# Tables, running-sum rows and spreads laid out with an outer dimension of eight in an attention and spectral-mix kernel

## The chip, the core and the metric

The kernel runs on one core of one Trainium2 chip. The metric is the device time of one execution in microseconds. The core has a matrix engine (TensorE, PE in the profile, with its weight loads as PEld), a vector engine (VectorE, DVE), an activation engine (ScalarE, ACT), GpSimd (POOL) and SyncE (SP), which computes nothing here and issues transfers. Transfers between DRAM, and within the on-chip memory (SBUF), are carried out by 16 DMA engines, which all queues share.

## The reference

Two layers follow each other. The first is causal attention with a learned decay, for 8 batches, 8 heads, 576 tokens and 64 values a head:

```python
scores = scale * np.matmul(q, k.transpose(0, 1, 3, 2))
cum = np.cumsum(np.maximum(s, 0.0), axis=-1)
bias = -(cum[:, :, :, None] - cum[:, :, None, :])
scores = np.where(causal, -1000000000.0, scores + np.minimum(bias, 0.0))
attn = softmax(scores)            # as max, exp, sum
x = np.matmul(attn, v)            # heads side by side: (8, 576, 512)
```

The second takes the Fourier transform of x along the tokens, keeps 64 modes, multiplies each mode by a complex 512 x 512 matrix of its own (`w_r`, `w_i`), transforms back and applies a last dense layer:

```python
X = np.fft.rfft(x, axis=1)
Yr = einsum('bmd,mde->bme', Xr, w_r) - einsum('bmd,mde->bme', Xi, w_i)
Yi = einsum('bmd,mde->bme', Xr, w_i) + einsum('bmd,mde->bme', Xi, w_r)
y = np.fft.irfft(Y, n=S, axis=1)
u = x + y
out = u + np.maximum(u @ w_ch, 0.0)
```

`w_r` and `w_i` together hold 2 x 64 x 512 x 512 values in float32, 134 MB, and are by far the largest input. The output is 8 x 576 x 512 in float32.

## The kernel before

**Attention and the stream of weights.** The 64 heads and batches are worked on in 32 steps of two heads of one batch (`n` from 0 to 31; `g, b = divmod(n, 8)`). A step transposes q and k on TensorE (`transposes`, L347), computes scores (`scores`, L381), their exponentials on ScalarE, the product with v (`av`, L416), and the forward transform of the result by a small matmul with a table (`fft`, L450). The decay enters through an additional row of the transposed q: row D of the tile `qt` holds minus eight times the running sum of `s` for the step's two heads, which meets a row of ones in `kt`.

The running sums are computed once, for all 64 heads and batches, by a scan on VectorE (L292) into `ncum_sb`, 64 partitions x 576 values in bfloat16. `cum_rows` (L336) brings two rows of them into `qt`, one transfer per step, issued by SP one step ahead. For steps 0 and 1 the row comes straight from `ncum_sb` (L345); for the other 30 it comes from a copy in DRAM, `ncum_dram`, which one transfer at L586 writes.

While attention runs, GpSimd issues the transfers of weights, q, k and v (`load`, L239, all at L243): they convert float32 to bfloat16 or float16 on the way. The weights come in pieces of 8 modes x 128 rows of the inner dimension, real and imaginary apart: `wq` lists them as (g, c, ri), four groups g of 128 rows, eight chunks c of eight modes, ri for real and imaginary. Each piece is two transfers of 512 KB as they arrive, one per half of the partitions. They land in two rings of buffers (`wpool`, `wpool2`), and at first in places that are used later for something else. At most eight of GpSimd's transfers are under way at a time: a semaphore is used again only after the transfer that held it has landed. `modes(g, c)` (L470) multiplies one chunk; it is called during attention for the first three groups, and after it for the last.

**After attention.** For the last group the eight chunks run one after the other (L862 to L897). `modes` returns the finished chunk as `yb`: 16 modes-by-parts (eight modes, real and imaginary) x 8 batches on the partitions, 512 columns. The inverse transform contracts over 128 modes-by-parts, so a chunk's rows must go to 16 partitions of the tile `yv`, with the batches side by side on them. For chunks 0 to 3 TensorE does this (`gather`, L717), and for the product with `w_ch` (`which` = 1) of chunks 4 and 5 and for both products of chunks 6 and 7 a transfer does: `spread` (L511). For chunks 4 and 5 the other product goes through `gather` as well. Its six calls are all issued by SP, in the order of chunks: chunk 4, chunk 5, chunk 6 (`which` 0 from L506, then 1 from L714), chunk 7 (L506 and L915).

The table of the inverse transform is `G_sb`, 128 x 576 in float16, loaded by SP at the start (L280). The last two chunks are not read from `yv` in the first pairs of output tiles: there `add_last` (L779) multiplies `yb` as it stands with a table spread over the partitions, `Gx_sb`, and `Gt_sb` for the last 64 tokens. SP loads `Gx_sb` (L634, one transfer) and `Gt_sb` (L638, four transfers) once attention is over.

While the last chunk is multiplied, `modes` is given work to put between its four parts (L897): before the third, `first_z` for two pairs of output tiles, which reads `yv` up to chunk 5; before the fourth, `first_u`. Then the output stage follows, a list of steps written out by hand (L953), which makes the 36 output tiles in 18 pairs; SP stores each pair as it is finished (L854, L857).

**What sets the order.** Each engine works through its own instructions in program order. SP's queue holds, in this order: the loads of `s` and the constants, the first rows of `qt`, the copy to `ncum_dram`, the 30 row transfers, `Gx_sb` and `Gt_sb`, the six spreads, the stores. What a transfer's layout decides is into how many pieces it is cut and over how many DMA engines they go.

## Time and profile before

| | us |
|---|---|
| median of 3 runs | 441.92 |
| lowest and highest | 440.32, 442.31 |
| profiled execution, own time | 442.11 |
| its span | 440.3 |
| PE busy | 340.8 (77%) |
| DVE busy | 252.5 (57%) |
| ACT busy | 226.0 (51%) |
| POOL busy | 171.7 (39%) |
| chain that ended last: share of DMA, PE, DVE | 53%, 25%, 15% |

The span is the time between the first and the last instruction of the profiled execution; 1.8 us lie around it. The page cuts the span in 40 slices of 11 us; a digit is the busy share of an engine in tenths, `PEclk` the share of the clock that TensorE was granted, `DMA` the mean busy share of the 16 DMA engines. In the table of queues, q0 holds what GpSimd issues, q1 what SP issues, q8 and q14 the fetching of the program itself; the columns are packets, megabytes and the time that the packets took as a share of 16 engines' span (a packet overlaps the next on its engine, so a share can pass 100%). The chain of waits starts at the last instruction and goes back at each step to what released it. Beside these views the trace keeps, for each DMA packet, its start, length, queue and size, and for each landing the times at which the transfer's semaphore was raised; a packet's engine is not recorded.

### The profile page before, as it was taken

How to read it: one execution, taken by the hardware profiler on the slowest of the kernel's cores; microseconds unless marked ns; L12 is line 12 of the kernel's file. 1: busy time of each engine (PE TensorE's matmuls, PEld its weight loads, DVE VectorE, ACT ScalarE, POOL GpSimd, SP SyncE). 2: the span in 40 equal slices, each digit the busy share in tenths (PEclk: the TensorE clock that was granted, in tenths of full speed). 3: DMA queues.
4: the chain of work that ended last, by engine and by line, in shares of the span. 5: the costliest groups of instructions: out<-in, count | busy, mean ns of one | idle time of the engine just before them, and what ended most of it. 6: DMA issues, size and time to landing. Idle time of an engine off the chain costs nothing.

```text
span 440.3 us, 10592 instructions
## 1 busy us (share of the span) xinstructions
PE 340.8 (77%) x4409; PEld 203.7 (46%) x4409; DVE 252.5 (57%) x574; ACT 226.0 (51%) x421; POOL 171.7 (39%) x257
## 2 busy tenths in 40 slices
PE   1588999899695977973939458899987797778995
PEld 1365666465463644641616125556554345432341
DVE  7667776677573555752715315766655344450795
ACT  1387878267463634860727024766651334330794
POOL 6555454424353444323444343433322212310293
PEclk9999999999988888995968767999999989996999
DMA  9999999999999999999999999999999999996498
GB/s 179 207 206 206 204 206 208 207 209 207 207 205 207 210 207 210 207 209 208 205 209 208 209 208 209 207 210 206 210 211 212 212 211 211 203 218 121 155 381 347
DMA packets 69063, 93.30 MB, mean 212 GB/s; under 512 B 25932, under 2 KB 27592, under 8 KB 69016
## 3 DMA queue, kind: packets, MB, share of 16 engines
q0 software_dynamic: 61424, 81.28, 104.6%
q1 hardware_dynamic: 7592, 11.36, 7.2%
q8 instruction: 34, 0.56, 0.5%
q14 instruction: 13, 0.11, 0.1%
HBM read 163.58 MB, written 9.51 MB: 393 GB/s over the span
## 4 chain that ended last, share of the span: by engine, by line
DMA 53%; PE 25%; DVE 15%; issue 3%; POOL 2%; ACT 1%; DVEq 0%; POOLq 0%
DMA w_sb<-in_moe_w_i_dram 21%; DMA w_sb<-in_moe_w_r_dram 17%; DMA qk<-in_k_dram 8%; DMA qk<-in_q_dram 5%; PE sc_ps L397 3%; DVE xs L468 3%; DVE qt L359 3%; PE z_ps L681 3%; PE yp L478 3%; DVE x_all L443 2%; PE av_ps L433 2%; PE sc_ps L391 2%; PE tr_ps L355 2%; DVE xt L553 2%; PE z_ps L773 2%
## 5 line engine op out<-in xcount | busy, mean ns | idle before, releaser
L405 ACT ACTIVATE p_sb<-sc_ps,cumt_sb 128x576 f16<-128x576 f32 (+1 forms) x256 | 141.9, 636 | 21.8 <-PE sc_ps L397 21.4
L397 PE MATMUL sc_ps<-qt,kt 128*128 128x512 bf16 (+2 forms) x384 | 76.8, 312 | 6.9 <-ACT kt L359 6.1
L243 POOL DMA_DIRECT2D v<-in_v_dram x72 | 51.4, 714 | 60.6 <-DMA w_sb<-in_moe_w_i_dram 12.8
L243 POOL DMA_DIRECT2D w_sb<-in_moe_w_i_dram x62 | 38.5, 623 | 89.2 <-DMA w_sb<-in_moe_w_i_dram 28.3
L359 DVE COPY qt<-tr_ps 64x576 bf16<-64x576 bf16 x64 | 47.8, 747 | 41.5 <-PE tr_ps L355 41.5
L478 PE MATMUL yp<-w_sb,xs 128*32 128x512 bf16 (+1 forms) x480 | 42.2, 431 | 29.1 <-DMA w_sb<-in_moe_w_i_dram 25.4
L355 PE MATMUL tr_ps<-ident,qk 64*64 64x64 bf16 x1152 | 34.3, 205 | 33.8 <-DMA qk<-in_k_dram 16.0
L243 POOL DMA_DIRECT2D w_sb<-in_moe_w_r_dram x60 | 37.4, 624 | 53.0 <-DMA w_sb<-in_moe_w_r_dram 33.3
L397 PEld LDWEIGHTS <-kt 128*128 128x128 bf16 x384 | 38.3, 105 | 34.5 <-ACT kt L359 12.8
L391 PE MATMUL sc_ps<-negm,ident 128*128 128x256 bf16 x256 | 53.5, 293 | 0.1
L355 PEld LDWEIGHTS <-qk 64*64 64x64 bf16 x1152 | 26.4, 117 | 51.7 <-DVE kt L359 20.3
L376 ACT ACTIVATE p<-sc_ps,cumt 128x64 f16<-128x64 f32 x32 | 10.1, 314 | 73.8 <-PE sc_ps L372 73.6
L433 PE MATMUL av_ps<-v,p_sb 128*128 128x65 f16 x1024 | 44.2, 197 | 1.8 <-DVE x_all L443 0.6
L359 ACT COPY kt<-tr_ps 64x576 bf16<-64x576 bf16 x32 | 22.8, 714 | 40.8 <-DVE qt L359 40.1
L433 PEld LDWEIGHTS <-p_sb 128*128 128x128 f16 x1024 | 37.4, 100 | 9.6 <-DVE x_all L443 5.4
L468 DVE CAST xs<-ft_ps 64x128 bf16<-64x128 f32 x128 | 36.7, 287 | 7.3 <-PE ft_ps L458 5.7
L478 PEld LDWEIGHTS <-xs 128*32 128x32 bf16 (+1 forms) x512 | 17.8, 146 | 46.0 <-DMA w_sb<-in_moe_w_i_dram 24.6
L438 DVE TENSOR_REDUCE den<-av_ps 128x5 f32<-128x10 f32 x64 | 10.8, 169 | 48.3 <-PE av_ps L433 47.3
L443 DVE TENSOR_TENSOR x_all<-av_ps,rcp 128x320 f16<-128x320 f32 x64 | 31.5, 492 | 2.2
L498 DVE TENSOR_TENSOR y_acc<-yp,y_acc 128x512 f32<-128x512 f32 x16 | 11.1, 692 | 29.2 <-PE yp L478 28.5
L539 ACT COPY z<-z_ps 128x512 f32<-128x512 f32 x22 | 12.9, 586 | 26.9 <-PE z_ps L571 14.2
L458 PE MATMUL ft_ps<-Ff_sb,x_all 128*64 128x192 f16 (+1 forms) x320 | 24.4, 266 | 1.0 <-DVE x_all L443 1.0
(107 smaller groups left out, 439.4 us busy)
## 6 DMA issues: line engine op xcount, KB each, us to landing
w_sb<-in_moe_w_r_dram POOLq DMA_DIRECT2D x60, 512.0 KB, 13.6
w_sb<-in_moe_w_i_dram POOLq DMA_DIRECT2D x55, 512.0 KB, 13.2
out_dram<-r_w SPq DMA_DIRECT2D x16, 512.0 KB
v<-in_v_dram POOLq DMA_DIRECT2D x72, 64.0 KB, 11.1
qk<-in_q_dram POOLq DMA_DIRECT2D x15, 288.0 KB, 12.0
qk<-in_k_dram POOLq DMA_DIRECT2D x15, 288.0 KB, 13.2
x_all<-in_moe_w_r_dram POOLq DMA_DIRECT2D x4, 512.0 KB, 8.4
w_sb<-in_moe_w_i_dram POOLq DMA_DIRECT2D x3, 384.0 KB, 12.7
```

The lines of the kernel that those rows point to most:

```text
L243: nc.gpsimd.dma_start(out=dst, in_=src)
L355: nc.tensor.transpose(ps[rows, r, :], src[rows, r, :], ident16[rows, rows])
L359: copy(out=to[:, :, :, half * RH : half * RH + RH], in_=ps[HP * i : HP * i + HP].rearrange("d r (h p) -> d h p r", h=2),)
L391: nc.tensor.matmul(ps[:, bass.ds(w * S, W)], ident16, negm[:, bass.ts(r, W)], start=True, stop=False, skip_group_check=True,)
L397: nc.tensor.matmul(ps[:, c0 : c0 + i1 - i0], keys[:, w, r, :], qh[:, i0:i1], start=False, stop=True, skip_group_check=True,)
L405: nc.scalar.activation(out=pt[:, poff[x] : poff[x] + S - w * W], in_=ps[:, w * S : (w + 1) * S - w * W], func=ACTF.Exp, bias=cumt_sb[:, x, ...
L433: nc.tensor.matmul(ps[:, I, r : r + NCH], lhsT, rhs, start=(i == 0), stop=(i == len(todo) - 1), skip_group_check=True,)
L443: nc.vector.tensor_tensor(out=x_all[:, g, b, :, D * h : D * h + D], in0=ps[:, :, 1 : NCH], in1=rcp.unsqueeze(2).to_broadcast([P, NT, D]), ...
L458: nc.tensor.matmul(ps[HP * q_ : HP * q_ + HP].rearrange("p h f -> p (h f)"), x_all[:nT, g, b, T, q_::2], Ff_sb[:nT, T, :], start=(T == 0), ...
L468: nc.vector.tensor_copy(out=xs[g % 2][HP * h : HP * h + HP, q_, :, h, :, b, :], in_=a)
L478: nc.tensor.matmul(ps[32 * cg : 32 * cg + 32, :], cols[k0:, q_, 1 - ri, :, c * MC // 2 + cg], wt[(g, c, ri)][cg // 2][k0:, 2 * (cg % 2) + ...
L681: nc.tensor.matmul(zs[i, x], xts[i][:, x, dt, :], wch_sb[:, dt, :], start=(dt == 0), stop=(last and dt == DT - 1), skip_group_check=True,)
```

## The change

Three kinds of transfers get another layout; what is computed stays the same.

- The three tables in DRAM (`c_Ginv`, `c_Ginvx`, `c_Ginvt`) are stored in eight parts with a gap between them, by a new function `eighths`. The source of their loads then has an outer dimension of 8, where it had 128 or 16 rows. The loads themselves are not edited.
- The copy of the running sums in DRAM is cut into four parts of 144 values per row, with a gap of 16 values after each. Its write has 64 x 4 pieces of 288 bytes for 64 of 1,152, and a step's row transfer reads 8 pieces of 288 bytes for two of 1,152.
- `spread` makes two transfers of 8 partitions each instead of one of 16, for all chunks but the last. There are then ten such transfers in place of six.

```diff
-    d_G = nc.inline_tensor(G_np, name="c_Ginv").ap()
+    def eighths(a, name):
+
+        n = len(a) // 8
+        t = np.zeros((8, n + 1) + a.shape[1:], a.dtype)
+        t[:, :n] = a.reshape((8, n) + a.shape[1:])
+        return nc.inline_tensor(t, name=name).ap()[:, :n]
+
+    d_G = eighths(G_np, "c_Ginv")
...
-    d_Gx = nc.inline_tensor(np.ascontiguousarray(Gx_np), name="c_Ginvx").ap()
+    d_Gx = eighths(Gx_np, "c_Ginvx")
...
-    d_Gt = nc.inline_tensor(np.ascontiguousarray(Gt_np), name="c_Ginvt").ap()
+    d_Gt = eighths(Gt_np, "c_Ginvt")
...
-    ncum_dram = dpool.tile([NPAIR, S + HP], BF16, name="ncum_dram")
+    NE8 = 8
+    CP = 2 * S // NE8
+    ncum_dram = dpool.tile([NPAIR, S // CP, CP + 16], BF16, name="ncum_dram")
...
-            nc.sync.dma_start(out=qt[n % NQ][D : D + 1, :, :], in_=ncum_dram[p0 : p0 + 2, :S].unsqueeze(0))
+            nc.sync.dma_start(
+                out=qt[n % NQ][D : D + 1, :, :],
+                in_=ncum_dram[p0 : p0 + 2, :, :CP].rearrange("h x t -> (h x) t"),
+            )
...
-        nc.sync.dma_start(out=yv[16 * c : 16 * c + 16, :, which, :], in_=rows)
+        n = 2 * MC if c == NCK - 1 else NE8
+        for r in range(0, 2 * MC, n):
+            nc.sync.dma_start(
+                out=yv[2 * MC * c + r : 2 * MC * c + r + n, :, which, :], in_=rows[B * r : B * (r + n), :]
+            )
...
-        nc.sync.dma_start(out=ncum_dram[:, :S], in_=ncum_sb)
+        nc.sync.dma_start(
+            out=ncum_dram[:, :, :CP], in_=ncum_sb.rearrange("c (x t) -> c x t", t=CP)
+        )
```

## The prediction

> **What bounds the kernel now.** I read the page first, its slices and its table of DMA queues:

> ```profile
> PEclk9999999999988888995968767999999989996999
> DMA  9999999999999999999999999999999999996498
> ...
> q0 software_dynamic: 61424, 81.28, 104.6%
> q1 hardware_dynamic: 7592, 11.36, 7.2%
> q8 instruction: 34, 0.56, 0.5%
> q14 instruction: 13, 0.11, 0.1%
> ```

> The 16 DMA engines are full in every slice up to about 396 us, while no compute engine is: the kernel is a stream of weights and q, k, v through queue q0, and the last weights set the end. Second, the chain of waits from 380 us on, in order of time, and the waits between 380 and 412 us:

> ```profile
> 383.57 15.64 DMA w_sb<-in_moe_w_r_dram
> 399.21 0.14 issue
> 399.35 1.09 PE yp L478 x6
> ...
> 406.55 0.60 PE yp L478 x4
> ```

> ```profile
> POOL w_sb L243 <- PE yt_ps L701: 13.2, 1, 13.2
> ...
> PE yp L478 <- DMA w_sb<-in_moe_w_r_dram: 1.9, 1, 1.9
> ```

> The real half of the last chunk lands at 399.21 us; TensorE has waited 1.9 us for it, and from 399.35 on it works without a gap to 406.55 and then through the output stage. So the landing at 399.21 is the one that counts, and a gain of more than 1.9 us there is worth nothing. Third, busy time by stretch; the columns are PE, PEld, DVE, ACT, POOL busy, granted clock, DMA share, GB/s:

> ```profile
> 382.00:400.00 18.00, 12.57 (x132) 5.79 (x132) 8.62 (x13) 3.83 (x7) 4.60 (x8) 0.95 1.11 211
> 400.00:406.00 6.00, 6.00 (x28) 1.63 (x22) 0.00 (x0) 0.00 (x0) 0.00 (x0) 0.57 0.44 91
> ```

> TensorE is full from 400 to 406 us, at a granted clock of 0.57.

> Fourth, below the page, the records of single DMA packets and of the semaphore increments with which each of the 16 engines reports a landing. A 2048-byte weight packet follows the last one on its engine after 154 ns. Summing such intervals, the engines are 98 to 101% used in each 5 us from 5 to 380 us, 92% from 380 to 385, when POOL waited for PE. So an engine's end is the sum of its work. But the engines aren't equal. For the transfer that POOL issued at 367.9 us, the 16 increments come, in ns after the first, at 0, 49, 80, 576, 902, 1230, 2446, 2558 and then at 3719, 3923, 4224, 4358, 4532, 4544, 4599, 4613: eight early engines, eight late ones. Each instruction fetch of 16 KB on q8 (0.9 to 1.3 us each, 33 before 405 us, in a cycle of eight recurring lengths) pushes one of the late ones back by 0.95 us; in the eight fetches from 293 to 390 us none pushes an early one. The row of running sums (two packets of 1152 bytes) pushes two engines back by some 60 ns each time; these are the early ones at 1230 and 2446 (A and B). I call the early one at 2558 C: it takes neither fetches nor rows. For the transfer that lands at 399.21, the last increment stands alone, 0.97 us after the next; B and C stand at 396.25 and 396.68 (which is which I can't tell), A at 395.5.

> **The change part by part.** It moves bytes between engines. These are the transfers touched:

> ```profile
> yv<-v_sb SPq DMA_DIRECT2D x4, 128.0 KB
> ...
> qt<-ncum_dram SPq DMA_DIRECT2D x30, 2.2 KB
> ...
> yv<-y_sb SPq DMA_DIRECT2D x2, 128.0 KB
> ...
> G_sb<-c_Ginv SPq DMA_DIRECT2D x1, 144.0 KB
> ncum_dram<-ncum_sb SPq DMA_DIRECT2D x1, 72.0 KB
> ...
> Ff_sb<-c_Ginvt SPq DMA_DIRECT2D x4, 4.0 KB
> ...
> Gx_sb<-c_Ginvx SPq DMA_DIRECT2D x1, 32.0 KB
> ```

> How many engines a transfer takes is read from its increments: 2 for a sum row, whose source has two rows; 16 for the others, whose outer dimension is 16 or more. The new outer dimension of 8 should give 8. Which eight, the trace can't show; I take the early ones, because the row's two engines are among them, and I bound it by the other case below (rival 2).

> Prices, from the interval between one q1 packet and the weight packet after it: 1152 bytes 60 ns, 1024 bytes 55 ns, 2048 bytes 93 ns, 256 bytes 27 ns, an increment 5 to 7 ns. For a packet of 288 bytes there is no row: between 27 ns (256 bytes) and 60 ns; I take 27, the nearest.

> - G table: 128 packets of 1152 bytes; 8 an engine before, 16 on eight engines after. Early +8 x 60 = +0.48 us, late -0.48.
> - Gx and Gt: one packet of 2048 and four of 256 bytes an engine. Early +0.19, late -0.19 (rounded down, together 0.2).
> - Spreads of chunks 4 and 5, whose packets run at 388 to 390 and 393.5 to 396 us: 8 x 55 ns each. Early +0.88, late -0.88. Those of chunk 6 run at 399 to 404 us, after the landing that counts; they weigh another 0.88 on the last weights.
> - 30 sum rows: A and B lose 30 x 60 = 1.8 us; all eight early engines gain 30 x (27 + 7) = 1.0 (up to 2.0 at 60 ns).
> - The sums' copy to DRAM: 64 packets become 256, 4 x 60 = 0.24 us an engine becomes 16 x 27 = 0.43: +0.19 on all 16 (+0.7 at 60 ns).

> Sum at the landing that counts: late -0.48 - 0.19 - 0.88 + 0.19 = -1.36, so 399.21 becomes 397.85. C +0.48 + 0.19 + 0.88 + 1.0 + 0.19 = +2.74, so 399.0 to 399.4. B 396.25 or 396.68 + 0.9, A less. The early engines that ran dry at 382 us keep that idle time as room. So C takes the place of the late engines, 0.2 us before to 0.2 after where they stood: the change shifts about 4.1 us between groups whose gap is 2.5. The landing is unmoved, and I take zero. The last weights land at 405.13; C then comes at 402.27 or 402.56 + 2.74 + 0.88 = 405.9 to 406.2, and TensorE asks for them at 406.48: hidden by 0.3 us, and if that cover goes, the excess counts one for one.

> **What hides the rest.** A sum row lands 3.9 us after its issue, and the scores that read it start 4.3 us (n = 2) to 25 us after that landing; eight packets on eight engines instead of two may add one weight packet's turn, 0.15 us. The copy to DRAM is asked for at 22.9 us, 15 us after its issue; its own packets end by 10 us. Chunk 5's spread, 16 packets an engine between weight packets, takes 16 x 0.209 = 3.3 us instead of 1.7 and is issued in two parts of 0.6 us: it ends at 398.1 instead of 395.8, and the matmul with the G table that reads it starts at 400.37. Uncovered it would cost up to 2.3 us. Chunk 6's last spread landed at 404.35; with 2.3 more it is 406.7, and the first matmul that reads it starts at 412.07. SP issues four more DMAs, 0.55 us each; behind them in its queue is only the spread of chunk 7 at 407.95, 9 us later. The output stage is not touched.

> [...]

> **Rivals.**

> 1. The balance gains. If C is not among the eight, or its lag goes with the change, the late engines decide: 397.85, 1.4 us earlier, 440.5 us. TensorE would then start before the half-clock stretch (398.3 to 405.2 us in the clock records, behind its 1.9 us of idling); if the stretch goes with the idling, 5.8 us of work shrink by up to 2.9: 437.6. For: the late engines really are relieved; against: C, and the last weights at 405.9, which would hold TensorE where it is now.
> 2. The eight engines hold some or all of the fetching ones (ends slower). Then the latest engine gets what I gave C: +2.74 at the landing that counts and 3.6 on the last weights, which land at 408.75 where TensorE asks at 406.48. That is 2.3 to 2.7 us: 444.2 to 444.6 us. It decides as soon as the engine that is last at 399.21 is among the eight. For: nothing in the trace numbers the engines; against: the row's two engines are both fetch-free.
> 3. Nothing reaches the path: what is moved is 0.8 MB of 93, and 16 engines drain the same total; 442 us. In numbers it can't be told from my forecast, only in the increments.
> [...]

> **How the numbers follow.** Forecast 0.37, rival 1 0.33, rival 2 0.15, rival 3 0.08, rival 4 0.07. The profiled execution took 442.11 us, its span 440.3 and 1.8 around it; the three runs shown have a median of 441.92 and reach from 440.32 to 442.31, so the span's sum is the median's within 0.2. Zero change gives 441.9. The forecast's own range is 441.2 to 442.6. 0.5%, 2.2 us, is about what a measurement of this kernel can tell from no change: the runs before spread by 2.0. Faster than that is the part of rival 1 in which some of the clock's gain comes too (0.25); slower is rival 2 and a little of rival 4 (0.17). The range takes in rival 1 with two thirds of the clock's gain, 440.5 - 1.9, and rival 2: 438.6 to 444.6.

> **What would show it.** In the profile after: 30 sum rows of 288-byte packets with eight increments each; the increments of one weight transfer at 380 us no longer in two groups 1 us apart but mixed, with the fetching ones 1.4 us earlier; the landing of the real half at 399.0 to 399.4; TensorE without a gap to about 406.5; chunk 5's spread before the G-table matmul. I am wrong if the late group moves back instead, if TensorE waits for the last weights near 406 or for a spread near 400, or if the half-clock stretch there goes or grows.

## The result, and the profile after

The changed kernel takes 445.03 us (median of 6 runs, 444.02 to 446.89), the kernel before 441.24 us on the same chip (440.32 to 442.31): a ratio of 1.0085, 95% interval 1.0067 to 1.0103. It is slower. The profiled execution took 445.12 us with a span of 443.1. Two more measurements of the same kernel, told below, gave 1.0070 (1.0043 to 1.0097) and 1.0065 (1.0043 to 1.0088).

The slices and the table of DMA queues of the changed kernel, with the columns of before:

```profile
PEclk9999999999887988995967768999998989996998
DMA  9999999999999999999999999999999999994498
...
q0 software_dynamic: 61424, 81.28, 103.9%
q1 hardware_dynamic: 8096, 11.36, 7.4%
q8 instruction: 34, 0.56, 0.5%
q14 instruction: 13, 0.11, 0.1%
```

The same bytes move, in 504 more packets on q1, and the engines are as full as before up to slice 36. Which engines do the work can't be read from these lines. The chain of waits of the changed kernel, in order of time (start, length, what):

```profile
384.60 15.76 DMA w_sb<-in_moe_w_r_dram
400.36 0.14 issue
400.50 1.08 PE yp L490 x8
...
407.38 0.60 PE yp L490 x4
...
408.79 5.08 DMA yv<-y_sb
413.86 0.14 issue
414.00 0.62 PE u_ps L791 x4
```

Two things differ from before. The landing that counts is 1.15 us later (400.36 for 399.21), and with it TensorE's work; and there is a new piece, 5.08 us of a transfer that stood in no chain before: chunk 7's spread, which TensorE now waits for. The waits between 380 and 416 us (total, times, longest) show both:

```profile
PE yp L490 <- DMA w_sb<-in_moe_w_r_dram: 2.1, 1, 2.1
...
PE u_ps L791 <- DMA yv<-y_sb: 1.6, 1, 1.6
...
PEld L490 <- DMA w_sb<-in_moe_w_i_dram: 1.2, 2, 0.8
```

Busy time by stretch of the changed kernel (PE, PEld, DVE, ACT, POOL, granted clock, DMA share, GB/s):

```profile
382.00:400.00 18.00, 12.31 (x128) 5.77 (x128) 8.88 (x14) 4.06 (x7) 4.84 (x8) 0.96 1.10 208
400.00:406.00 6.00, 5.50 (x25) 1.50 (x26) 0.00 (x0) 0.00 (x0) 0.00 (x0) 0.54 0.51 106
```

TensorE starts at 400.50, and these 0.50 us are all that it lacks in a stretch that it filled before; from there on it is busy without a gap, as before. The granted clock there is 0.54 for 0.57.

Below the page, the semaphore increments of one weight transfer each that was issued near 368 us, in ns after its first. The second line is the before that the prediction read:

```
before                 0   49   80  576  902 1230 2446 2558 3719 3923 4224 4358 4532 4544 4599 4613
after                  0  174 2134 2233 2303 2858 3518 3903 4623 4634 4675 4698 4798 4829 6397 6446
```

Most of the case is in these two lines. After the change there are four groups: two engines that nothing was moved to (0, 174), six that got work and had room for it (2134 to 3903), six that were relieved (they end at 386.8 to 387.0 us, the late ones of before at 386.6 to 387.5), and two alone, 1.6 us behind all others. Six and two make the eight engines of the new layouts: a row's landing now has eight increments where it had two, and so has one of Gx, of Gt and of a moved spread, where it had 16. I followed the packets of single engines from interval to interval between 88 and 190 us of this trace: two engines that get every row of sums in 288-byte packets there also carry instruction fetches, at 110.4 and 119.2 us; the other six row engines carry none. I call these two the pair. Its fetches last 893 and 892 ns, two of the cycle's eight lengths (974, 975, 961, 893, 892, 948, 945, 935 at places 0 to 7), and I use the length as the engine's name in the other traces; that is a reading, no trace names an engine.

The increments show the same without following packets. The next fetches of these two lengths start at 304.7 and 313.4 us. In the last transfers that land before 305 us the last increment comes at most 5.0 us after the first, with others close by; in the one that lands at 308.5 us one increment stands alone at 6.05, and in the one that lands at 316.9 us a second has joined it (6.09 and 6.26). So the two lone engines are the ones that take the fetches of 893 and 892 ns. They are still alone at the landing that counts, where chunk 4's and chunk 5's spreads have been added: there the last two increments are 1.68 us behind all others, and in the two further traces of the changed kernel (E5, E16) 1.07 and 1.55 us. In the kernel before a single one is alone, by 0.97 us, and in its second trace (E13) none by more than 0.4.

### The profile page after: what moved, and what is told of

Read it like the earlier page. It is cut to its first block, busy times and chain, and to the rows that moved or that the text cites. A ratio compares the mean times of both kernels' runs of the same rounds, so it can differ in the third digit from the quotient of the medians.

```text
span 443.1 us, 10602 instructions
## 1 busy us (share of the span) xinstructions
PE 342.6 (77%) x4409; PEld 205.0 (46%) x4409; DVE 252.5 (57%) x574; ACT 226.1 (51%) x421; POOL 171.7 (39%) x257
## 3 DMA queue, kind: packets, MB, share of 16 engines
q0 software_dynamic: 61424, 81.28, 103.9%
q1 hardware_dynamic: 8096, 11.36, 7.4%
## 4 chain that ended last, share of the span: by engine, by line
DMA 45%; PE 27%; DVE 17%; issue 4%; ACT 3%; POOL 3%; DVEq 0%; POOLq 0%; ACTq 0%
DMA w_sb<-in_moe_w_r_dram 20%; DMA w_sb<-in_moe_w_i_dram 16%; DMA qk<-in_k_dram 5%; PE yp L490 4%; DVE qt L371 4%; PE sc_ps L409 4%; DVE xs L480 3%; DMA qk<-in_q_dram 3%; PE z_ps L699 3%; PE av_ps L445 2%; PE tr_ps L367 2%; PE sc_ps L403 2%; DVE x_all L455 2%; DVE kt L371 2%; PE z_ps L791 2%
## 5 line engine op out<-in xcount | busy, mean ns | idle before, releaser
(107 smaller groups left out, 441.9 us busy)
## 6 DMA issues: line engine op xcount, KB each, us to landing
qk<-in_k_dram POOLq DMA_DIRECT2D x15, 288.0 KB, 13.2
```

## Experiments

In each, "theory T" ("theory A" in E1 to E4) is that the pair sets the end: it has the fetches, and the change puts the rows, the tables and the spreads on top. No kernel leaves any computation out; E4 and E7 have transfers that nobody reads, and E6 and E7 make a few products twice.

**Each part alone (E1, E2, E3).** The edits are the three parts of the change:

```diff
 # E1: the layout of ncum_dram, its write and the row transfers, as changed
 # E2: spread() alone
+        n = 2 * MC if c == NCK - 1 else 8
+        for r in range(0, 2 * MC, n):
 # E3: eighths() for c_Ginv, c_Ginvx, c_Ginvt alone
```

> Only the sum rows and their copy in DRAM take the new layout; tables and spreads stay as before. Theory A (two of the eight engines are among those that fetch instructions): those two gain 30 x 34 ns + 0.19 = 1.2 us and stand out at 380 us; the landing of the last real half moves later by 0.2 to 1.0 us, the time by +0.3 to +1.2 us. Theory B (the eight are fetch-free and the loss comes from the small packets themselves): all eight move alike, no pair stands out, and this kernel alone has most of the 3.8 us.

> Only the spreads of chunks four to six are split in two. Theory A: two fetching engines get +0.88 us before the landing of the last real half and +1.76 on the last weights: the landing moves by 0 to +0.5 us, the time by 0 to +1 us, more only if the chunk-7 spread runs into an instruction fetch near 410 us as in the changed kernel (then +1.5 more). Theory C (the spreads themselves are late: two issues, twice the packets an engine): TensorE waits for a spread before 408 us, and this kernel alone has most of the 3.8 us.

> Only the three tables are in eight parts. Theory A: two fetching engines get +0.67 us, the six others -0.67: the landing of the last real half moves by -0.5 to +0.2 us, the time by -0.5 to +0.3 us. Theory D (the table at the start delays the first q, k and v): the first steps, up to 30 us, are later by some 0.5 us and the time with them.

Rows 1.0002 (0.9990 to 1.0015), spreads 1.0023 (1.0008 to 1.0039), tables 1.0001 (0.9989 to 1.0013). The landing that counts came at 399.91, 400.56 and 398.57 us. Not all of this was expected: with the rows the time stayed where it was, where at least 0.3 us more had been expected; with the spreads the landing came 1.35 us later instead of 0.5 at most (the fetch near 390 us, of the 893 ns class, falls on one of the pair there, see E14 below); with the tables it came 0.64 us earlier instead of 0.5 at most. The parts add up to 0.26%, where the whole costs 0.65 to 0.85%. The tables show the pair: at 368 us two increments stand 0.66 and 1.04 us behind the next. With the rows alone there is no such gap, the last four stand within 0.13 us. I read it so: the pair stood in the late group with some room to its top, and the 1.1 us of the rows lift it to the top and little further. How much room, the whole change tells: by its prices the pair gets 2.0 us (rows 1.1, copy 0.19, tables 0.67), and the last increment near 367 us moves by 1.08 to 1.33 in the three traces told below; the difference, 0.7 to 0.9 us, is the room. It is worked out against the first trace of before; where the last increment stands depends on the place in the fetch cycle too (it is 0.8 us later in E13), and of the three traces two (the first and E5, +1.08 and +1.13) have the same place as that one.

**Marks (E4).** The kernel before with three unread transfers from DRAM to DRAM, with outer dimensions of 4, 6 and 8 and 20 packets of 1,920 bytes per engine, after steps 14, 18 and 24:

```diff
+            if n in marks:
+                src = moe_w_ch.rearrange("(k r) e -> k r e", k=8)[: marks[n], :20, :480]
+                nc.sync.dma_start(out=mark_dram[n][:, :, :480], in_=src)
```

> The kernel before with three additional transfers from DRAM to DRAM that nobody reads, issued by SP in steps 14, 18 and 24, with an outer dimension of 4, 6 and 8 and 20 packets of 1920 bytes for each. Each pushes the engines that it takes back by about 2 us, which the increments of the weight transfers show. Theory A: of the eight engines that the third pushes back, exactly two also take fetches; the first (4 engines) and perhaps the second (6) take none of them. Theory B: the third pushes no fetching engine. Its time is of no interest.

444.74 us in a single run. It settles nothing: the marks pull the increments apart to 6 us with no groups left (0, 311, 504, 1016, 1954 and so on up to 6064), and I could not say which engine was which.

**Two parts at a time (E9, E10, E11), and rows for four engines (E12).** E9 has rows and tables, E10 rows and spreads, E11 spreads and tables, each as in the change. E12 is the changed kernel with one number altered:

```diff
-    CP = 2 * S // NE8
+    CP = 2 * S // 4
```

> The changed kernel with its spreads put back on 16 engines (rows and tables changed). Theory T (two fetch-taking engines among the eight, the pair, set the end; rows, tables and spreads add up on them, and up to some point the room in front of the latest engine swallows it): the pair has the rows and the tables, so the last increment of the transfer issued near 366 us is 0.9 to 1.2 us later than before, as in the changed kernel; it has 0.88 us less at the landing of the last real half and 1.76 less at the last weights. Landing 399.2 to 400.0, last weights 405.1 to 406.0, time 0 to 0.4% over before. Rival (each part costs what it costs alone, and the parts add up): 0.03% over before. Rival 2 (the rows are what costs, once something else has taken the room): as the changed kernel, 0.7 to 0.85%.

> The changed kernel with its three tables as before (rows and spreads changed). Theory T: the pair has the rows (1.1 us with the copy) and the spreads (0.88 us at the landing, 1.76 at the last weights) but not the tables' 0.67: last increment at 366 us 0.3 to 0.6 later than before, landing 400.3 to 401.1, last weights 406.9 to 407.8, time 0.4 to 0.8% over before. Rival (the parts add up): 0.25%.

> The changed kernel with its rows and their copy as before, on two engines (spreads and tables changed). Theory T: the pair has the tables (0.67) and the spreads but not the rows: last increment at 366 us 0.1 to 0.4 later than before, landing 399.6 to 400.6, last weights 406.3 to 407.3, time 0.2 to 0.5% over before. Rival (the parts add up): 0.24%, which is inside that; the increments decide, not the time.

> The changed kernel with one number altered: the rows of sums lie in pieces of 576 bytes, four to a row pair, so that a row goes to four engines instead of eight; the copy to DRAM has 128 packets instead of 256. Tables and spreads as changed. If the pair is not among the first four (as the tables at four had it, with no lone increments), the pair is rid of the rows, 1.0 us, and nothing else is altered for it. Theory T: last increment at 366 us only 0.1 to 0.4 later than before instead of 1.1, landing 0.6 to 1.0 us earlier than in the changed kernel, time 0.15 to 0.25% under the changed kernel, about that of spreads and tables alone (0.2 to 0.5% over before). Rival (what the rows bring is spread over all eight engines or comes through SP's queue): as the changed kernel, 0.7 to 0.85% over before, with the increments as there.

| | ratio, 95% interval | last increment near 367 us, against before | landing that counts | last weights |
|---|---|---|---|---|
| E9 rows, tables | 1.0022 (1.0008 to 1.0036) | +1.47 | 399.77 | 405.69 |
| E10 rows, spreads | 1.0052 (1.0033 to 1.0071) | +0.41 | 399.67 | 406.27 |
| E11 spreads, tables | 1.0067 (1.0042 to 1.0092) | +1.68 | 401.79 | 408.30 |
| E12 rows for four | 1.0042 (1.0025 to 1.0059) | +0.07 | 400.54 | 406.52 |
| all three parts | 1.0085, 1.0070, 1.0065 | +1.08 | 400.36 | 406.90 |

E9 came out as theory T has it, in the landing, the last weights and the time; its last increment moved 0.3 us more than expected. E10's time is within what it gave, but its landing and last weights were 0.6 us earlier. E12 is the cleanest near 367 us: the same rows for four engines instead of eight, and the last increment is back at +0.07 us (+1.08 with eight); the gap behind the rest shrinks from 1.6 to 0.8 us, about what the tables alone make. So there the rows' share sits on engines that the layout with eight takes and the layout with four does not, and the rival, that all eight or SP's queue pay for the rows, falls. The time falls by 0.23 to 0.43% of before against the changed kernel, at the edge of what the intervals can part. The landing missed: 400.54 us is not the 0.6 to 1.0 us earlier that was expected but within the 400.36 to 401.09 of the changed kernel's three traces, and there three increments stand within 0.45 us of each other instead of a lone pair. What sets E12's landing stays open. E11 missed: 401.79 where 399.6 to 400.6 was expected, and the increments were late. Its trace has one difference that I had not looked for: the fetch near 390 us.

**The same kernels again (E13 to E16).** Nothing is altered in these four; they give a second trace of before, of E2 and of E11, and a third of the changed kernel (the second, E5, belongs here too).

> The changed kernel once more, with nothing altered, for a second trace. Theory T (two of the eight engines also take instruction fetches; I call them the pair): the trace after, against the one before, has its last increment of the transfer issued near 368 us 1.08 us later, the real half of the last chunk lands 1.15 us later, and a second loss follows: the spread of chunk 7, issued at 408.79, has one engine at 413.86 where the others end by 411.61, beside an instruction fetch at 410.19, and TensorE waits 1.58 us. If both belong to the change, a second trace has the two lone last increments 1.3 to 1.7 us behind the rest at 370 us, a landing of the real half at 399.9 to 400.8, and TensorE's wait for the spread of 1 to 2 us, and a median of 444.5 to 445.5. Rival (the second loss is a matter of 0.2 us of timing in one execution): the second trace has the pair but not the wait, and a median near 443.5.

> The kernel before once more, nothing altered, for a second trace. In the first trace TensorE was the one that set the end of the weight stage (last product with weights at 406.75 us, the last weights landed at 405.13). I expect the fetch cycle at the same start (the fetch near 390 us of 974 ns class, not one of the pair's 893), the landing of the real half at 398.5 to 399.5, the last weights at 404.5 to 405.5 and the last product at 405 to 406.8, time ratio 0.999 to 1.001.

> Only the spreads on eight engines, as run before, nothing altered, for a second trace. The first had the fetch near 390 us on one of the pair (893 ns class), two lone last increments at 5.65 and 6.19 us and a landing of the real half at 400.56. If the start of the fetch cycle belongs to the program: the same again, 0.1 to 0.4% over before. If it belongs to the execution: most likely another start, then the landing is at 399.3 to 400.0 and no lone increment is over 1.3 us behind the others.

> Spreads and tables on eight engines, rows on two, as run before, nothing altered, for a second trace. The first had the fetch near 390 us on one of the pair, a landing of the real half at 401.79, last weights at 408.30 and 0.67% over before, where I had expected 399.6 to 400.6, 406.3 to 407.3 and 0.2 to 0.5%. If the start of the fetch cycle belongs to the execution: another start now, and the landing within what I had expected. If to the program: the same start, landing 401.3 to 402.2, 0.5 to 0.8%.

> The changed kernel a third time, nothing altered. The lone pair 1.4 to 1.7 us behind the others at 370 us, last increment 1.0 to 1.2 us later than before, landing of the real half 400.2 to 401.2, last weights 406.8 to 407.6, time 0.6 to 0.9% over before. For the wait on the spread of chunk 7 I have no expectation: it comes when the fetch near 410 us starts less than 0.5 us after the first packets of the spread (0.19 us in the trace with the wait, 0.87 in the one before).

First the fetches. These are the lengths, in ns, of those from about 304 us on (start in us); some after 389 us, when packets of the spreads run as well, are longer (1201 at 390.6):

```
E11 spreads+tables        305.4 948  314.0 945  322.9 935  335.7 975  353.6 975  373.5 961  390.6 1201
E15 spreads+tables again  304.5 935  313.1 974  321.9 974  334.6 962  352.9 893  371.9 893  389.0 948
```

The cycle's next length after 961 is 893, so in E11 the fetch at 390.6 is on one of the pair; in E15, the same program, both of the pair's fetches came earlier and the one at 389 us is on another engine. The chain of waits of E15 shows the landing:

```profile
382.30 17.36 DMA w_sb<-in_moe_w_r_dram
399.66 0.14 issue
399.80 1.09 PE yp L485 x8
```

399.66 for 401.79, and 1.0041 (1.0023 to 1.0060) for 1.0067: what E11 was expected to be, but for last weights 0.4 us earlier (405.91). One fetch is about 0.95 us of these 2.13. Near 367 us, before the fetches near 390, the last increments of the two traces already stood 1.25 us apart (+1.68 and +0.43), so the fetch near 390 us is not all of it, and I can't divide it further. Where the cycle starts belongs to the execution. Its first fetch had place 1, 1 and 6 in the three traces of the changed kernel, 1 and 2 in those of before, 3 and 5 in those of E11. E14 had place 3 again, as E2 had, the pair's fetch at 390.0, a landing at 401.05, one increment 1.6 us behind the next in the transfer that counts, and 1.0037 (1.0018 to 1.0055). TensorE's longest wait for a DMA in E14:

```profile
PE yp L478 <- DMA w_sb<-in_moe_w_r_dram: 3.1, 1, 3.1
```

Next, the changed kernel and before. The chain of E5, the changed kernel again:

```profile
389.19 18.26 DMA w_sb<-in_moe_w_i_dram
407.45 0.04 issue
407.49 0.67 PE yp L490 x4
```

and of E13, before again:

```profile
382.69 16.77 DMA w_sb<-in_moe_w_r_dram
399.47 0.14 issue
399.60 1.08 PE yp L478 x6
...
406.02 0.60 PE yp L478 x4
```

In E5 it is the very last weights that TensorE waits for; in E13, as in the first trace of before, they were there in time (405.31). The five traces side by side, in us; the last columns are the start of TensorE's last matmul with weights, from there to the issue of the last store, and from that to the end of the span:

| | landing that counts | last weights | last matmul with weights | output stage | closing | span |
|---|---|---|---|---|---|---|
| before | 399.21 | 405.13 | 406.75 | 29.52 | 4.08 | 440.35 |
| E13, before again | 399.47 | 405.31 | 406.22 | 29.52 | 4.07 | 439.81 |
| after | 400.36 | 406.90 | 407.58 | 31.18 | 4.34 | 443.10 |
| E5, after again | 401.09 | 407.45 | 407.76 | 29.52 | 4.34 | 441.62 |
| E16, after again | 401.01 | 407.36 | 408.59 | 29.53 | 4.33 | 442.45 |

The means differ by 2.31 us: 1.49 up to the last matmul with weights, 0.55 in the output stage (all of it in one trace) and 0.26 in the closing. The closing is 4.06 to 4.09 in all traces without the changed spreads that add nothing else (before, E1, E3, E8, E9) and 4.31 to 4.34 in all with them that add nothing else; SP has four transfers more there. The medians of the timed runs differ by 2.9 to 3.8 us, more than the traces: both traces of before are of executions 0.2 to 0.9 us slower than before's medians, and that of E5 is one of the faster of its kernel.

The pair stands alone in all three traces of the changed kernel: the last two increments near 366 us are 1.6, 1.4 and 1.2 us behind the next one. In E13 it is not so: three stand together 0.65 us behind. The last increment by itself says less: in E13 it is 0.8 us later than in the first trace of before.

The wait for chunk 7's spread came in one trace of three. Where it came, the timeline of the changed kernel has (start, length, engine, line, what, idle before and its releaser)

```profile
411.79 0.62 PE L821 MATMUL u_ps<-x_all,ident16h 64*64 64x512 f16 x4
414.00 0.62 PE L791 MATMUL u_ps<-yv,G_sb 128*64 128x512 f16 x4 [1.58 <-DMA yv<-y_sb]
```

and 15 of the spread's increments by 411.61 us and one at 413.86. An instruction fetch of 1,719 ns starts at 410.19, 0.15 us after the spread's first packets; in the first trace of before it starts 0.71 us after them, and the spread's last increment is at 410.99. The other traces bear this out: in E15 the fetch starts 0.20 us after the first packets, the last increment is 0.80 us behind the other fifteen, and TensorE waits 0.2 us for it; in all the rest the fetch starts 0.43 to 0.87 us after them, or before the spread is issued (E6, E7), and the last increment is at most 0.17 us behind. So it is a matter of timing of a few tenths of a microsecond, which later weights can bring about; how often it comes in the timed runs is open.

**The last fetch moved (E6), and the rows twice (E7).** E6 is the changed kernel with 24 short matmuls more in the last six steps of attention, to shift where the program's instructions are fetched: the trace of before has 34 fetches for 8,818 matmuls and weight loads, one for every 259. E7 is E6 with each row transferred a second time into DRAM.

```diff
 # E6, in first_transposed
+        if x == 0:
+            for dt in range(DT):
+                nc.tensor.matmul(
+                    ps[:, dt, :16], x_all[:, dt, b, T, :], ident16h[:, :16], start=True, stop=True,
+                    skip_group_check=True,
+                )
 # E7, in addition
+            nc.sync.dma_start(
+                out=row_copy[n], in_=ncum_dram[p0 : p0 + 2, :, :CP].rearrange("h x t -> (h x) t")
+            )
```

> The changed kernel with 24 short matmuls more (16 columns each, the first sixteen columns of a transpose that is made anyway, four in each of the last six steps of the attention). They compute nothing new. TensorE's instructions are fetched every 256 or so of them, so 48 more (weight load and matmul) should make the last fetch come 48 instructions earlier in the program: at 405.5 to 407 us instead of 410.19, before the spread of chunk 7 is issued. Theory T with the collision as a cause: TensorE's wait of 1.58 us for that spread goes, the rest of the loss stays: landing of the real half 399.9 to 400.8, time 1.2 to 1.7 us under the unaltered changed kernel, 443.3 to 443.9. Rival 1 (the spread is late because its own engines are behind with other packets): the wait stays at 1 to 2 us, 445. Rival 2 (what was lost is lost somewhere else, the wait only shows it): the wait goes and the time stays within 0.5 us of 445.

> The kernel of the run before (24 short matmuls more), with each of the 30 rows of sums moved a second time, from the same source, in eight pieces, into a place in DRAM that nobody reads. It doubles what the rows give to each of the eight engines: 30 times 32 ns and an increment of 5 to 7 ns, 1.1 us an engine. Theory T (the pair sets the end): its last increments at 370 us fall back by another 1.0 to 1.3 us, to 2.5 to 3 us behind the rest, the real half lands 0.9 to 1.3 us later than in the run before, and the time grows by 0.9 to 1.5 us. Rival (the fetch-free early engines, which I had feared in the prediction, or all 16 alike through the copy to DRAM, set the end): the six fetch-free ones of the eight move by 1.1 us within their 3 us of room, the landing and the time stay within 0.3 us.

E6 took 445.63 us (1.0100, 1.0079 to 1.0122), slower than the changed kernel next to it (444.10). The fetch did move, to 406.3 us, and no wait for the spread is left; but neither had E5 that wait, so E6 says nothing on its share. What it shows is another thing. The cycle started at place 3, and the fetch at 387.46 (893 ns) fell on one of the pair: from one transfer to the next the last increment jumps from 6013 to 8100 ns (0.88 of that is chunk 4's spread, by its price), and the landing that counts is at 402.31. The chain of E6 there is

```profile
391.15 17.08 DMA w_sb<-in_moe_w_i_dram
408.23 0.04 issue
408.27 0.67 PE yp L490 x4
```

Its closing is 5.60 us for 4.34, with a 35th fetch of 1,313 ns at 431.5 in the midst of the stores; the other traces told of so far have none after 413 us within their span. E7 took 447.13 us (1.0131, 1.0110 to 1.0152), 1.5 us more than E6. The last increment near 367 us fell back by 1.8 us against E6, more than the 1.0 to 1.3 expected, to 2.3 us behind the rest (the other of the pair stands 1.4 us behind, about as in E6). The landing did not follow (402.28 for 402.31): E7's cycle started at place 6, so that its pair had one fetch less. Of the 1.29 us between the two spans 0.51 is up to the last matmul with weights and 0.79 in the closing. So E7 bears theory T out at 367 us for one of the pair, and at the end the two effects can't be parted.

**The tables for four engines (E8).** The kernel before, with the tables alone, cut into four:

```diff
+        n = len(a) // 4
+        t = np.zeros((4, n + 1) + a.shape[1:], a.dtype)
```

> The kernel before, with only the three tables of the inverse transform laid out with an outer dimension of four instead of 16 or more. By the prices of the prediction four engines get 24 x 60 ns + 0.57 us = 2.0 us more, the other twelve 0.67 us less. Theory T says only that two of the first eight engines take fetches. Case a (the two are not among the first four): no lone increments at the end; the late group is relieved as a whole by 0.6 us, the real half lands at 398.4 to 398.9 (before: 399.21), time 441.0 to 441.6. Case b (one or both are among the first four): one or two lone increments 1.5 to 2.5 us behind the others at 370 us, landing 400.5 to 401.5, time 442.8 to 444. With the tables at eight the trace had two increments 0.65 and 1.04 us behind the others.

No increment stands 1.5 us or more behind (5,809 and 5,828 ns, the next at 5,289), and the landing is at 398.53: case a, no sign of a fetching engine among the four. In the transfer issued near 368 us four increments are early (0 to 537 ns, the next at 3,384) where before has eight, as it should be if the four that got the tables come out of the early ones. But the last increment near 367 us is 0.2 us later than before, not 0.6 earlier, and the time did not follow: 442.47 us, 1.0027 (1.0011 to 1.0043) where at most 441.6 was expected. Its trace is of the fastest of its ten runs and shows no cause; this stays open. No version came out faster than the kernel before.

## Why the prediction was wrong, point by point

**What bounds the kernel: right.** The landing of the last real half, and behind it the last weights, set the end; both moved, and the time with them.

**The step that failed** is "Which eight, the trace can't show; I take the early ones, because the row's two engines are among them". Two engines that are fetch-free say little about the six that come with them. Of the eight that the new layouts take, six carry no fetch between 88 and 190 us and two do (893 and 892 ns); among the two of a row before, and the four of E8 and E12, none was seen. So the sum "late -1.36, C +2.74" was made for the wrong engines: the six late ones that the change doesn't touch were relieved by about the 0.5 us that had been worked out for 367 us, but the end belongs to the two that it loads: against the prediction's 0, the landing moved by 1.15 to 1.88 us. No run numbers the engines.

**Rival 2 was what happened**, in its mechanism: "the eight engines hold some or all of the fetching ones". I gave it 0.15 and 444.2 to 444.6 us; the medians are 444.10 to 445.03. Its parts were off, in both directions. It put +2.74 us on the landing and +3.6 on the last weights; measured are +1.2 to +1.9 and +1.8 to +2.3. The difference is the room: the pair was not last before. It stood some 0.7 to 0.9 us from the top of the late group, and at the landing that counts the last engine of before stood 0.97 us alone, about what one fetch pushes an engine back (0.95 us): the fetch at 390 us, which did not fall on the pair in the changed kernel's traces. On the other side I held "the output stage is not touched": it costs 0.26 us more in closing in every trace, and 1.66 us in one of three through the spread of chunk 7. The range ended at 444.6; the first median lies 0.4 us above it, the two repeats within it.

**The prices were nearly right.** Following packets stand 32 ns apart for 288 bytes, where I took 27: 30 rows give 1.1 us an engine with their increments instead of 1.0. 288 bytes in 32 ns are 9 bytes per ns, 1,152 in 60 ns are 19.

**What hides the rest: right** up to chunk 7. Chunk 5's spread, worked out at 398.1 us, landed in its two parts at 398.07 and 399.91, so its end was 1.8 us later than worked out (by 0.6 because the prediction took 395.8 us for its end before, where the last increment is at 396.42), and the first matmul that reads it started at 401.51, 1.6 us after it; chunk 6's landed at 407.10 (406.7 worked out) and was not waited for. What was not costed is chunk 7's spread, which the change does not touch: it was covered only where an instruction fetch came 0.43 us or more after its first packets, or before it was issued; at 0.15 us its last increment was 2.25 us behind the others, at 0.20 us 0.80.

**Fewer engines for a transfer:** the moved spreads did take longer on eight, in two parts: the packets of chunk 4's start within 4.2 us instead of 2.2, those of chunk 5's within 3.6 instead of 2.0 (3.3 and 1.7 were worked out). But that is not where the time went, since nobody waits for these: the one spread that is waited for is chunk 7's, and the change leaves that as it was. It is the sum of what is put on the fullest engines that counts: the pair's last increment near 367 us comes 1.08 us after the last one of before, and the landing is 1.15 later.

**Why the parts do not add up** follows from the room: rows, tables or spreads alone fit into 0.7 to 0.9 us or nearly so (0.02, 0.23 to 0.37, 0.01%), two together cost 0.22 to 0.67%, and all three 0.65 to 0.85%. The three measurements of the whole, taken together, are clear of the sum; those of two parts are not, or barely. The reading by the room is borne out by the increments of E3, E9 and E12 near 367 us; for E10 and E11 the place of the fetches weighs as much as the parts do, and at the landing E12 does not show it.

## What to carry to other kernels

With the 16 DMA engines full here, laying transfers out for eight of them cost 0.65 to 0.85%, as two of the eight carry instruction fetches too and came last, 1.68 us behind all others at the landing that counts: find out which engines they are before working out a balance, from the increments and the fetches as above, or by one run with a single such transfer (not tried here; E4, with three in one run, settled nothing). An engine's slack is the distance between its last increment and the latest one at the transfer that counts; here the rows or the tables alone, below it, cost 0.02 and 0.01%, and all three parts together 0.65 to 0.85%, where the parts add up to 0.26. And a second trace of the same kernel comes first when an effect is as small as this: here two executions of one program (E11, E15) had landings 2.13 us apart, about 0.95 us of it one instruction fetch.
